# Front of an attention and feed-forward kernel: copies of v, weight passes and evictions placed anew, and ten unread products at the start

## The chip, the cores and the metric

The kernel runs on one NeuronCore of a Trainium2 chip. The metric is device time in microseconds (us) for one execution, from the first to the last instruction and a little around it. Less is better.

## What is computed

The reference is a thresholded attention, and behind it a feed-forward block with the SoLU activation:

```python
scores = (q @ k.T) / sqrt(64)                        # 8 batches, 8 heads, 576 x 576
thresh = max(scores, axis=-1) - tau                  # tau = 0.02
scores = where(scores >= thresh, scores, -1e9)
attn = softmax(scores)
x = (attn @ v)  ->  4608 tokens x 512
h = x @ w_in                                         # 512 x 1024
solu = h * softmax(h)
out = (layernorm(solu) * g_ln) @ w_out               # 1024 x 512
```

q, k and v are fp32. The weights w_in and w_out come as 64-bit floats, and the kernel turns them into fp32 itself.

## The kernel before

The kernel is one long program without loops on the chip; Python loops write it out. It goes in rounds. A round has one slot of the attention: 128 query rows against 576 keys, for each of two heads. Batch b has 18 slots (four pairs of heads, two kinds of rows and two halves of each, and two slots for the last 64 rows), so there are 144 rounds. Rounds 0 to 29 are the front; from round 30 (START) a steady order follows that works off attention and feed-forward side by side.

In a round, TensorE makes the scores into two PSUM tiles, s0 and s1, of which there is one each, so the scores of a round wait until ScalarE has read those of the round before. VectorE takes the row maxima (`maxes`, L526), ScalarE makes everything below the threshold vanish with a steep ramp (`ramp`, L541) and takes exponentials with row sums (`exps`, L550). In the round after, GpSimd divides by the sums (`normalise`, L557 to L560), VectorE transposes blocks of 32x32 (`blocks`, L571), and the SyncE queue moves the blocks into place (`spread`, tile wT, L592 to L601). Some rounds later TensorE multiplies them with v (L631); ScalarE copies the result to xh (L664).

Around this the front does three things:

- **The weights.** They come in 16 pieces (0 to 7 of w_in, 8 to 15 of w_out). Each goes through `weight_load` (into one of four raw buffers, RAW), `weight_a` (an exponent pass on the engine that UNIT names: 0 VectorE, 1 ScalarE, 2 GpSimd, L294 to L298; a sign pass on VectorE, L303; a low-word pass on ScalarE, L306), `weight_b` (VectorE, L318) and `weight_c` (an addition on GpSimd, L328). The pieces of w_out are also scaled by g_ln (`weight_gain`, engine by GAIN: 0 ScalarE, 1 VectorE, 2 GpSimd) and copied to swapped rows (`weight_d`, engine by MOVER: 0 ScalarE, 1 VectorE, 2 GpSimd, 3 a DMA).
- **q, k and v.** Each pair of heads of batches 0 and 1 is turned on TensorE by products with an identity (`turn`, L372) and evicted from PSUM. PREP says in which round the items of pairs 4 to 7 are turned, and EASED whether ScalarE does all the evictions of a round (1) or shares them with VectorE (0). Pairs of later batches are loaded in their natural form (LOAD2), transposed by VectorE (TURN2, L221) and moved by DMAs (L223). The rows of v of batch 0 are copied once to the other half of the partitions, in eight copies (`copy_v`; VAT says when, VBY on which engine: 0 ScalarE, L187; 1 VectorE; 2 GpSimd, L191). FETCH and V2 say when q, k and v are loaded.
- **Four tiles of the feed-forward block** in rounds 11 to 32 (HO gives the rounds of their products, CHAIN the places of the steps between: maximum, exponential, product, statistics, normalising in two halves, the swap DMAs, the transpose).

Each engine works through its instructions in the order of the program. That order is set by hand: a time in VAT, PIECE or MOVE is 4 times the round plus a phase. Phase 0 is before the scores of the round, 1 before the normalising, 2 before the feed-forward and attention products and the transposes, 3 at the round's end. `weigh` runs what is due at a phase; at one phase the additions come first, then `weight_b`, loads, `weight_a`, scalings, copies of weights, copies of v. In CHAIN a step has one of four places (begin, early, middle, late) and a number of rounds after its products.

A product with v becomes due three rounds after the second slot of its unit, plus LAG. Due ones stand in a list in order. In the front one is taken from its head in a round, under this condition, where `what` names the feed-forward steps of the round:

```python
if due and "o" not in what and len(pairs_free) > ("h" in what and steps[0][1] == 0):
    attending = pv_due.pop(0)[1]
```

The beginning is its own: the first loads, the constants, then the turning of pair 0 (k, a quarter of q and the ends) by `turned`, and round 0.

Of the kernel before, what the change touches and what calls it, by code (L numbers as in the profile page):

```python
# [8 lines left out]
F32 = mybir.dt.float32  # L9
# [11 lines left out]
def kernel(  # L21
# [937 lines left out]
    SPLIT = {30: 0, 32: 30, 34: 6, 36: 5, 38: 16, 40: 30, 42: 7, 44: 23, 46: 11}  # L959
    LATER, KEPT = 47, (3, 4)  # L960
    SEVEN = {0: 21, 1: 21, 2: 24, 3: 25, 5: 25, 4: 26, 7: 26, 6: 29}
    PIECE = {0: (-1, 1, 3, 6, 7, ), 1: (-1, 3, 5, 10, 11, ), 2: (-1, 8, 11, 14, 15, ), 3: (3, 12, 15, 18, 19, ), 4: (4, 15, 18, 21, 25, ), 5: (7, 20, 23, 26, 27, ), 6: (11, 23, 25, 30, 31, ), 7: (13, 27, 31, 34, 35, ), 8: (23, 31, 35, 38, 39, ), 9: (23, 35, 39, 42, 43, ), 10: (29, 39, 43, 46, 47, ), 11: (35, 43, 47, 50, 51, ), 12: (39, 49, 51, 54, 55, ), 13: (43, 52, 55, 58, 59, ), 14: (43, 55, 59, 62, 63, ), 15: (55, 59, 63, 66, 67, )}
# [4 lines left out]
    MOVER = {16: 0, 17: 0, 18: 2, 19: 1, 20: 2, 21: 0, 22: 3, 23: 3, 24: 0, 25: 0, 26: 3, 27: 3, 28: 3, 29: 2, 30: 3, 31: 3}  # L967
    MOVE = {8: 47, 9: 55, 10: 55, 13: 63, 14: 70, 15: 67}
    EASED = {0: 0, 1: 1, 2: 1, 3: 1, 4: 1, 5: 1, 6: 1, 7: 0, 8: 1, 9: 1, 10: 0, 11: 1, 12: 0, 13: 0, 14: 0, 15: 1, 16: 1, 17: 0, 18: 0, 19: 1, 20: 1, 21: 0}
    SECOND = {0: 0, 1: 1, 2: 0, 3: 1, (1, 0, 0): 1}  # L970
    PREP = {0: 14, 1: 14, 2: 14, 3: 15, 4: 15, 5: 17, 6: 16, 7: 16, 8: 19, 9: 19, 10: 18, 11: 20, 12: 20, 13: 22, 14: 21, 15: 21}
    LAG = {1: 2, 3: 1, 5: 1, 9: 1, 11: 1, 17: 0, 21: 0, 23: 1, 25: 1}
    FETCH = {0: 10, 1: 8, 2: 8, 3: 11, 4: 15, 5: 15, 6: 13, 7: 17, 8: 17, 9: 19, 10: 21, 11: 25, 12: 0, 13: 0, 14: 3, 15: 5}
# [3 lines left out]
    LOAD2 = {0: 20, 1: 17, 2: 24, 3: 21, 4: 31, 5: 31, 6: 32, 7: 34}  # L977
# [338 lines left out]
    with tc.manual_schedule():  # L1316
# [317 lines left out]
```

## Time and profile before

| | before |
|---|---|
| three runs | 845.42, 846.64, 848.91 us |
| median | 846.64 us |
| the profiled execution | 848.12 us |
| its span, first to last instruction | 846.3 us |
| mean granted TensorE clock | 0.983 |
| busy: TensorE, VectorE, ScalarE, GpSimd | 799.6, 674.5, 605.0, 574.2 us |

In the lines of the profile, PE is TensorE's matmuls, PEld its weight loads, DVE VectorE, ACT ScalarE, POOL GpSimd, SP SyncE, and a q behind the name is the engine's queue. A line of a timeline has the start and the duration in us, engine, source line, operation, the tile written and those read, the shape, the count, and in brackets how long the engine stood idle before it and what ended that. A matmul in fp32 counts as two. A line of the page about an engine's 40 slices shows the busy tenths of each.

### The profile page before, as it was taken

Reading aid. Unit: us, or ns where it says so; the run is one execution under the profiler, and the core shown is the slowest. Engines: PE = TensorE matmul, PEld = TensorE weight load, DVE = VectorE, ACT = ScalarE, POOL = GpSimd, SP = SyncE. Lnnn points to the kernel's source line nnn. Section 1 sums busy time; section 2 is a strip of 40 time slices with the busy share of each in tenths; the row PEclk is TensorE's granted clock in tenths of the full one; section 3 lists DMA queues with packets and bytes.
Section 4 is the critical chain, followed back from the end, with each engine's and each line's share of the span. In section 5 each row is a group of like instructions: output and inputs, shape, how many; then the busy total and the mean of one; then the engine's idle time right before and its main releaser. Section 6 shows DMA issues by size and latency. Waiting matters only on the chain.

```text
span 846.3 us, 36895 instructions
## 1 busy us (share of the span) xinstructions
PE 799.6 (94%) x15345; PEld 554.4 (66%) x15345; DVE 674.5 (80%) x1323; ACT 605.0 (71%) x1218; POOL 574.2 (68%) x1036
## 2 busy tenths in 40 slices
PE   5569889999999999999999999999999999999997
PEld 3346667766665666666777876666676876666556
DVE  5799869878789698979798698979688888787362
ACT  6799868767777686878686787778586687876231
POOL 4979767866867667677766768686666768574330
PEclk9789999999999999999999999999999999999999
DMA  8989788988787687968787677877687666555122
GB/s 252 256 219 253 189 204 212 236 222 211 220 244 216 174 224 211 242 190 218 205 230 208 195 207 220 231 206 199 192 218 222 180 183 201 150 138 139 42 52 52
DMA packets 99768, 166.40 MB, mean 197 GB/s; under 512 B 18504, under 2 KB 47184, under 8 KB 99600
## 3 DMA queue, kind: packets, MB, share of 16 engines
q1 hardware_dynamic: 98688, 162.95, 71.1%
q8 instruction: 121, 1.98, 1.0%
q10 hardware_dynamic: 912, 1.08, 0.5%
q14 instruction: 47, 0.39, 0.1%
HBM read 45.09 MB, written 9.44 MB: 64 GB/s over the span
## 4 chain that ended last, share of the span: by engine, by line
PE 82%; ACT 5%; POOL 3%; DMA 3%; issue 3%; DVE 2%; SPq 1%; DVEq 0%; POOLq 0%; ACTq 0%
PE ov L1195 22%; PE h L747 17%; PE s_ps L504 15%; PE ov L631 13%; PE o_ps L1195 6%; PE h L771 5%; ACT w L541 2%; PE h_ps L1061 2%; DMA wT<-T 2%; DMA v<-in_v_dram 1%; ACT w L550 1%; POOL w L560 1%; PE pv L631 1%; DVE w L526 1%; PE s_ps L372 1%
## 5 line engine op out<-in xcount | busy, mean ns | idle before, releaser
L541 ACT ACTIVATE w<-s_ps,nth 128x576 f32<-128x576 f32 x282 | 199.6, 741 | 141.4 <-DVE nth L526 136.2
L526 DVE CUSTOM_DVE_ANT_0 w<-s_ps,tau_t 128x576 f32<-128x576 f32 x282 | 201.4, 750 | 51.8 <-PE s_ps L504 40.7
L560 POOL TENSOR_SCALAR w<-w,sm 128x576 f32<-128x576 f32 x288 | 214.6, 757 | 14.3
L1195 PE MATMUL ov<-w,uT 64*64 64x256 f32 x3456 | 220.5, 379 | 2.8 <-issue 2.8
L571 DVE STREAM_TRANSPOSE T<-w 128x576 f32<-128x576 f32 x288 | 207.4, 755 | 19.2 <-POOL w L560 18.4
L550 ACT ACTIVATE w<-w,ntau 128x576 f32<-128x576 f32 x288 | 219.7, 768 | 0.0
L504 PE MATMUL s_ps<-kT,qT 64*64 64x512 f32 (+1 forms) x2048 | 174.8, 418 | 20.1 <-ACT w L541 17.9
L1195 PEld LDWEIGHTS ov<-w,uT 64*64 64x64 f32 x3456 | 158.3, 134 | 49.1 <-issue 13.6
L631 PEld LDWEIGHTS ov<-wT,v 64*64 64x64 f32 x4752 | 132.6, 133 | 33.5 <-issue 18.7
L631 PE MATMUL ov<-wT,v 64*64 64x128 f32 (+1 forms) x4752 | 137.6, 259 | 0.2
L557 POOL TENSOR_SCALAR sm<-sm 128x2 f32<-128x2 f32 x144 | 45.9, 319 | 134.9 <-ACT w L550 130.3
L558 POOL TENSOR_TENSOR sm<-sm,mone 128x2 f32<-128x2 f32 x144 | 103.5, 719 | 12.0
L504 PEld LDWEIGHTS s_ps<-kT,qT 64*64 64x64 f32 x2048 | 72.0, 137 | 51.0 <-ACT w L541 23.7
L747 PE MATMUL h<-w,xh 64*64 64x512 f32 x832 | 103.4, 593 | 0.5 <-POOL mark L110 0.4
L1150 DVE TENSOR_SCALAR u<-u,rs,nb 128x1024 f32<-128x1024 f32 x31 | 29.8, 961 | 49.6 <-ACT V L1144 49.6
L1195 PE MATMUL o_ps<-w,uT 64*64 64x256 f32 x1088 | 65.5, 377 | 0.8 <-ACT xh L664 0.5
L747 PEld LDWEIGHTS h<-w,xh 64*64 64x64 f32 x832 | 38.6, 133 | 40.5 <-issue 23.1
L1195 PEld LDWEIGHTS o_ps<-w,uT 64*64 64x64 f32 x1088 | 49.1, 133 | 19.1 <-issue 5.2
L550 ACT ACTIVATION_READ_ACCUMULATOR w<-w,ntau 128x1 f32 x288 | 55.7, 193 | 0.0
L1177 DVE STREAM_TRANSPOSE uT<-V 128x1024 f32<-128x1024 f32 x36 | 44.0, 1221 | 14.2 <-DMA V<-u 4.9
L747 PE MATMUL h<-k,sum 64*64 64x512 f32 x312 | 50.6, 589 | 0.0
L1144 ACT ACTIVATE V<-u,nb,rs 128x1024 f32<-128x1024 f32 x36 | 44.7, 1241 | 5.2 <-POOL nb L1122 5.2
(134 smaller groups left out, 1017.0 us busy)
## 6 DMA issues: line engine op xcount, KB each, us to landing
wT<-T SPq DMA_DIRECT2D x132, 288.0 KB, 4.8
wT<-T SPq DMA_DIRECT2D x256, 144.0 KB, 4.0
out_dram<-ob SPq DMA_DIRECT2D x71, 128.0 KB, 4.3
V<-u SPq DMA_DIRECT2D x136, 64.0 KB, 2.0
wT<-T SPq DMA_DIRECT2D x14, 576.0 KB, 5.5
q<-in_q_dram SPq DMA_DIRECT2D x24, 288.0 KB, 4.6
q<-in_k_dram SPq DMA_DIRECT2D x24, 288.0 KB, 4.5
v<-in_v_dram SPq DMA_DIRECT2D x12, 576.0 KB, 5.6
```

Of the source, the lines that this page charges most:

```text
L504: nc.tensor.matmul(out=ps[h][ROWS[y], ks], lhsT=lhsT, rhs=d["kT"][ROWS[h], ks], start=True, stop=True,)
L526: nc.vector.tensor_tensor_reduce(out=w, in0=ps[:, 0:S], in1=(zero if loose else tau_t).to_broadcast([P, S]), scale=1.0, scalar=BIG, op0=AL ...
L541: nc.scalar.activation(out=d["w"][x], in_=d["w"][x] if d["loose"] else d["ps"][x][:, 0:S], func=AF.Prelu, bias=d["nth"][x], scale=-1.0, al ...
L550: nc.scalar.activation(out=w, in_=w, func=AF.Exp, bias=ntau, scale=1.0, accum_out=sm[:, x : x + 1])
L557: nc.gpsimd.tensor_scalar(out=sm, in0=sm, scalar1=1e-9, scalar2=None, op0=ALU.add)
L558: nc.gpsimd.tensor_tensor(out=sm, in0=sm, in1=mone, op=ALU.pow)
L560: nc.gpsimd.tensor_scalar(out=w, in0=w, scalar1=sm[:, x : x + 1], scalar2=1.0, op0=ALU.mult, op1=ALU.mult)
L571: nc.vector.transpose(out=T[:, :, r, :, h, :], in_=w.rearrange("p (c m x) -> p c m x", c=2, x=32))
L631: nc.tensor.matmul(out=to, lhsT=d["v"][ROWS[u], (h0 + h - u) % 4 if b > 1 else h0 + h, m ^ 4 * u if m < 8 and b < 2 else m,], rhs=rhs, sta ...
L747: mm = nc.tensor.matmul(out=h[ROWS[y], 512 * bank : 512 * bank + 512], lhsT=x[ROWS[r], ROWS[y]], rhs=w[ROWS[r]], start=c == 0 and (n, r, k ...
L1144: nc.scalar.activation(out=V, in_=u, func=AF.Identity, bias=nb, scale=rs)
L1195: nc.tensor.matmul(out=to[ROWS[z], 0:256], lhsT=d["uT"][ROWS[r], m].rearrange("p y x -> p (y x)"), rhs=w2[ROWS[r], m ^ r, 256 * z : 256 * ...
```

## The change

Nothing is computed otherwise, and no instruction of the attention or the feed-forward block is added or taken away. The tables that place the front's side work get other values, and ten products are added at the start. Part by part:

- **Ten unread products.** VectorE clears a tile of 128x128 ahead of the constants (in a buffer of tag T). TensorE multiplies it with itself, into s0, seven times ahead of the first turning and three times between the first turning and the scores of round 0. Nobody reads the results.
- **Copies of v.** Copies 0 to 7 stood at times 15, 15, 19, 19 (GpSimd) and 31, 31, 34, 34 (ScalarE). Now 0 and 2 are VectorE's at the beginning of rounds 3 and 4, 1 is ScalarE's in round 2, 3 stays GpSimd's in round 3, 4 is GpSimd's at the end of round 8, and 5, 6 and 7 are ScalarE's in rounds 8, 7 and 8.
- **Weight passes.** The exponent passes of pieces 0, 14 and 15 go from VectorE to GpSimd, those of 6 and 8 from ScalarE to GpSimd, that of 5 from GpSimd to VectorE, that of 11 from ScalarE to VectorE. The scaling of piece 8 goes from VectorE to GpSimd, that of 9 from ScalarE to VectorE, that of 10 from VectorE to ScalarE. One swapped-row copy goes from ScalarE to GpSimd (21) and one from GpSimd to ScalarE (29). Several passes change their phase: the addition of piece 1 goes ahead of the normalising of round 1, the passes b of pieces 3, 5, 8 and 11 ahead of the transposes of their rounds, the load of piece 6 from round 2 to 3, of piece 10 from round 7 to 6, and the copies of pieces 8, 9 and 10 some phases forward.
- **q and k.** Two items of pair 5 are turned in rounds 13 and 14 instead of 15 and 17, one of pair 6 in round 21 instead of 18, one of pair 7 in round 19 instead of 20. Rounds 15, 16, 19 and 20 share their evictions between ScalarE and VectorE; round 13 has them on ScalarE.
- **Loads.** The loads of k of pair 5 and q of pair 4, of v of batch 1 (second half, 21 to 25) and of batch 2, and the natural loads and transposes of batch 2 move by some rounds.
- **Products with v.** LAG makes those after slots 3, 11, 21 and 23 due two, two, one and two rounds earlier.
- **The chains of the first feed-forward tiles.** Some steps move by one place or one round; the store of the first goes from round 19 to 21, the swap of the second's halves from round 20 to the end of 19, and the transpose of the fourth from round 31 to 32.

```diff
+    BEFORE, BESIDE = 7, 3
...
-    UNIT = {0: 0, 1: 2, 2: 2, 3: 2, 4: 1, 5: 2, 6: 1, 7: 1, 8: 1, 9: 0, 10: 1, 11: 1, 12: 1, 13: 1, 14: 0, 15: 0}
-    GAIN = {8: 1, 9: 0, 10: 1, 11: 0, 12: 2, 13: 0, 14: 0, 15: 2}
+    UNIT = {0: 2, 1: 2, 2: 2, 3: 2, 4: 1, 5: 0, 6: 2, 7: 1, 8: 2, 9: 0, 10: 1, 11: 0, 12: 1, 13: 1, 14: 2, 15: 2}
+    GAIN = {8: 2, 9: 1, 10: 0, 11: 0, 12: 2, 13: 0, 14: 0, 15: 2}
...
-    VAT = {0: 15, 1: 15, 2: 19, 3: 19, 4: 31, 5: 31, 6: 34, 7: 34}
-    VBY = {0: 2, 1: 2, 2: 2, 3: 2, 4: 0, 5: 0, 6: 0, 7: 0}
+    VAT = {0: 12, 1: 9, 2: 16, 3: 15, 4: 35, 5: 32, 6: 29, 7: 34}
+    VBY = {0: 1, 1: 0, 2: 1, 3: 2, 4: 2, 5: 0, 6: 0, 7: 0}
...
+        rest = work.tile([P, 2, 2, NK, 2, 32], F32, tag="T", name="rest")
+        still = rest.rearrange("p c r m h x -> p (c r m h x)")[:, 0:P]
+        nc.vector.memset(still, 0.0)
+        idle = ps_mm.tile([P, 1024], F32, tag="s0", name="idle")
+
+        def idle_products(n):
+            for _ in range(n):
+                nc.tensor.matmul(
+                    out=idle[:, 0:P], lhsT=still, rhs=still, start=True, stop=True
+                )
+
+        idle_products(BEFORE)
         constants()
...
         turned(first, [k_item(0), q_item(0, slice(0, 1)), e_item(0)])
+        idle_products(BESIDE)
```

The other tables, old to new, only the entries that differ (a piece with all five times: load, a, b, c, scaling; the copies have the fifth time too, or that of MOVE):

```text
PIECE  1: (-1,3,5,10,11) -> (-1,3,5,9,11); 3: (3,12,15,18,19) -> (3,12,14,18,19)
       5: (7,20,23,26,27) -> (7,20,21,26,27); 6: (11,23,25,30,31) -> (13,24,25,30,32)
       8: (23,31,35,38,39) -> (23,31,34,38,39); 10: (29,39,43,46,47) -> (27,39,43,46,47)
       11: (35,43,47,50,51) -> (35,43,46,50,51); 12: (39,49,51,54,55) -> (39,50,51,55,55)
       13: (43,52,55,58,59) -> (43,51,54,56,56)
MOVE   8: 47 -> 43; 9: 55 -> 53; 10: 55 -> 52        MOVER  21: 0 -> 2; 29: 2 -> 0
EASED  4, 8, 15, 16, 19, 20: 1 -> 0; 10, 13: 0 -> 1
PREP   4: 15 -> 13; 5: 17 -> 14; 10: 18 -> 21; 12: 20 -> 19
LAG    3: 1 -> -1; 11: 1 -> -1; 21: 0 -> -1; 23: 1 -> -1
FETCH  1: 8 -> 9; 2: 8 -> 11; 10: 21 -> 25; 15: 5 -> 6
LOAD2  0: 20 -> 18; 1: 17 -> 20; 5: 31 -> 29; 6: 32 -> 29; 7: 34 -> 35
TURN2  1: 24 -> 25; 3: 28 -> 30; 4: 33 -> 34; 5: 34 -> 38
V2     0: 21 -> 22; 1: 27 -> 24; 2: 32 -> 37; 3: 35 -> 40
CHAIN  2: (3,1) -> (0,2); 9: (3,1) -> (3,3); 13: (3,3) -> (2,3); 16: (1,6) -> (3,5);
       19: (0,1) -> (1,1); 25: (3,2) -> (0,3); 29: (3,1) -> (2,2); 32: (3,1) -> (1,1);
       37: (1,6) -> (3,7); 39: (2,2) -> (3,1)
```

More of the change, by code (lines that the diff above doesn't have):

```diff
@@ L970 @@
+    MOVE = {8: 43, 9: 53, 10: 52, 13: 63, 14: 70, 15: 67}
+    EASED = {0: 0, 1: 1, 2: 1, 3: 1, 4: 0, 5: 1, 6: 1, 7: 0, 8: 0, 9: 1, 10: 1, 11: 1, 12: 0, 13: 1, 14: 0, 15: 0, 16: 0, 17: 0, 18: 0, 19: 0, 20: 0, 21: 0}
     SECOND = {0: 0, 1: 1, 2: 0, 3: 1, (1, 0, 0): 1}
-    PREP = {0: 14, 1: 14, 2: 14, 3: 15, 4: 15, 5: 17, 6: 16, 7: 16, 8: 19, 9: 19, 10: 18, 11: 20, 12: 20, 13: 22, 14: 21, 15: 21}
-    LAG = {1: 2, 3: 1, 5: 1, 9: 1, 11: 1, 17: 0, 21: 0, 23: 1, 25: 1}
-    FETCH = {0: 10, 1: 8, 2: 8, 3: 11, 4: 15, 5: 15, 6: 13, 7: 17, 8: 17, 9: 19, 10: 21, 11: 25, 12: 0, 13: 0, 14: 3, 15: 5}
+    PREP = {0: 14, 1: 14, 2: 14, 3: 15, 4: 13, 5: 14, 6: 16, 7: 16, 8: 19, 9: 19, 10: 21, 11: 20, 12: 19, 13: 22, 14: 21, 15: 21}
```

16 lines of the change are left out of this document (8 added, 8 removed).

## The prediction

> **What bounds the kernel now.** I read first the page: its span, its busy shares and its 40 slices.
>
> ```profile
> span 846.3 us, 36895 instructions
> PE 799.6 (94%) x15345; PEld 554.4 (66%) x15345; DVE 674.5 (80%) x1323; ACT 605.0 (71%) x1218; POOL 574.2 (68%) x1036
> PE   5569889999999999999999999999999999999997
> ```
>
> TensorE is busy 94% of the span, and all of its idleness that can be won back is in the first four slices (85 us). The change touches rounds 0 to about 40 only, most of it rounds 0 to 22, so the question is how much sooner the front hands over to a stretch in which TensorE is already full. Second view: the windows, by engine.
>
> ```profile
> 30.00:40.00 10.00, 6.02 (x76) 3.97 (x78) 5.60 (x12) 8.55 (x21) 9.21 (x14) 0.66 0.88 235
> 50.00:60.00 10.00, 6.25 (x104) 4.26 (x104) 9.04 (x19) 9.88 (x21) 7.36 (x10) 0.83 0.86 216
> 140.00:150.00 10.00, 10.00 (x198) 7.17 (x194) 8.70 (x16) 7.59 (x15) 9.38 (x13) 1.00 0.60 135
> 150.00:160.00 10.00, 10.00 (x204) 8.98 (x199) 8.26 (x17) 7.34 (x15) 8.85 (x16) 1.00 1.06 248
> ```
>
> The columns behind the width are PE, PEld, DVE, ACT, POOL, granted clock, DMA share, GB/s. From 30 to 40 us GpSimd is the full engine (9.21) and VectorE is idle by nearly half; from 50 to 60 ScalarE is full (9.88); from 140 on it is TensorE. Three stretches, three limits.
>
> Third view: the timelines of rounds 1 to 7, engine by engine. In a round the ramp on ScalarE (L541) waits for the maxima (L526) on VectorE, these for the scores (L504) on TensorE, and the scores for the ramp of the round before, which frees their banks. VectorE runs in order, and ahead of the maxima of round r+1 it has the transposes (L571) of round r-1, which wait for GpSimd's normalising (L557 to L560).
>
> ```profile
> 24.68 1.42 ACT L541 ACTIVATE w<-s_ps,nth 128x576 f32<-128x576 f32 x2
> 34.53 1.41 ACT L541 ACTIVATE w<-s_ps,nth 128x576 f32<-128x576 f32 x2
> 42.55 1.42 ACT L541 ACTIVATE w<-s_ps,nth 128x576 f32<-128x576 f32 x2 [4.01 <-DVE nth L526]
> 38.82 1.50 DVE L571 STREAM_TRANSPOSE T<-w 128x576 f32<-128x576 f32 x2 [3.75 <-POOL w L560]
> 41.71 0.74 DVE L526 CUSTOM_DVE_ANT_0 w<-s_ps,tau_t 128x576 f32<-128x576 f32 x1
> 27.68 1.69 POOL L191 TENSOR_SCALAR v<-v 64x512 f32<-64x512 f32 x2
> 33.52 1.35 POOL L191 TENSOR_SCALAR v<-v 64x512 f32<-64x512 f32 x2
> 34.95 0.65 POOL L298 TENSOR_SCALAR em<-raw 128x512 f32<-128x512 f32 x1
> 35.99 2.19 PE L504 MATMUL s_ps<-kT,qT 64*64 64x64 f32 x12 [0.15 <-ACT w L541]
> ```
>
> The ramps of rounds 3, 5 and 6 start at 24.68, 34.53 and 42.55: round 6 is 8.0 us after round 5, where rounds 3 to 5 took 4.9 each. Round 6 had its scores by 38.2 (35.99 + 2.19), but its maxima began at 41.71, behind transposes that stood 3.75 us for GpSimd, and that was late because it had copied v four times (1.69 + 1.35) and run a weight pass (0.65) since 27.68.
>
> **The start (ten products).** Seven products of 128x128 run while TensorE waits for k, three while it waits for the first evictions.
>
> ```profile
> 3.58 1.19 PE L372 MATMUL tp<-ident,k 64*64 64x64 f32 x31 [3.58 <-DMA k<-in_k_dram]
> 6.19 2.20 PE L504 MATMUL s_ps<-kT,qT 64*64 64x64 f32 x16 [0.98 <-DVE kT L451]
> 48.30 1.24 PE L504 MATMUL s_ps<-kT,qT 64*64 64x64 f32 x16
> 12.79 0.92 DVE L303 TENSOR_SCALAR em<-raw 128x512 int32<-128x512 int32 x1 [1.53 <-DMA raw<-in_moe_w_in_dram]
> 10.11 0.42 DVE L303 TENSOR_SCALAR em<-raw 128x512 int32<-128x512 int32 x1
> 15.07 1.45 ACT L541 ACTIVATE w<-s_ps,nth 128x576 f32<-128x576 f32 x2
> ```
>
> The same 16 scores take 2.20 us in round 0 and 1.24 in round 8, so a TensorE that is at full clock by 6.2 us saves up to 0.96; one that is not saves nothing, and the products may then delay the first turning (idle until 3.58) by some tenths. I take 0.5 gained, bounds 1.0 gained to 0.4 lost. It gets through to the ramp of round 1 (15.07), but no more than 0.6 would: the maxima of that round stand behind a pass that waits for raw weights until 12.79 and takes 0.92, so the first of them (0.74) is done at 14.4 at best. The Trainium skill ("TensorE: Matmul & The Clock Gate", What's actually happening) says the clock follows activity in free-running windows of about 3.4 us, whatever the kernel's start. By that the gain would be 0 or nearly 1 from run to run, and one run cannot tell which; the two L504 rows agree with a clock of half and of full.
>
> **Rounds 2 to 5, a loss.** The addition of weight piece 1 on GpSimd (L328) moves ahead of the normalising of round 1, and a copy of v each goes to VectorE ahead of the maxima of rounds 3 and 4.
>
> ```profile
> 18.72 0.23 POOL L557 TENSOR_SCALAR sm<-sm 128x2 f32<-128x2 f32 x1
> 21.30 1.28 POOL L328 TENSOR_TENSOR w<-w,em 128x512 int32<-128x512 int32 x1
> 23.83 0.74 DVE L526 CUSTOM_DVE_ANT_0 w<-s_ps,tau_t 128x576 f32<-128x576 f32 x1
> ```
>
> Normalising runs from 18.72 to 21.30; 1.28 in front make that 22.6. VectorE then still has one transpose (0.75), the scaling and sign passes it had before (together 1.7, from 22.1 to 23.83), and a copy, which I price as the nearest VectorE pass, 0.42 alone, 0.92 beside GpSimd: 22.6 + 0.75 + 1.7 + 0.42 = 25.5 for the maxima instead of 23.83, and the ramp of round 3 about 26.2 instead of 24.68, 1.5 later. ScalarE has its copy of v (0.62, half of the row at 51.19 below) in that hole. v should be there: its load is issued at 14.26 and such loads land in 5.6 us. In rounds 4 and 5 the loop recovers a little; I carry 1.2 late at the ramp of round 5 (bounds 0.5 and 2.0).
>
> ```profile
> 14.26 0.37 SPq L174 DMA_DIRECT2D v<-in_v_dram  x1
> v<-in_v_dram SPq DMA_DIRECT2D x12, 576.0 KB, 5.6
> 51.19 1.25 ACT L187 COPY v<-v 64x512 f32<-64x512 f32 x2
> 49.95 0.67 ACT L294 ACTIVATE em<-raw 128x512 f32<-128x512 f32 x1
> ```
>
> **Round 6, the gain.** GpSimd loses three of four copies and the pass of piece 5: 1.69 + 1.35 + 0.65 less about 0.75 for the copy that stays is 2.9, less the 1.3 of above that it starts late. Its normalising of round 4 then ends ahead of the scores of round 6 and is no longer what is late. Late is the loop itself: ramp of round 5 at 34.53 + 1.2 = 35.7, done at 37.1, scores 2.2 at half clock to 39.3, first maximum 0.7, ramp at 40.0 instead of 42.55. Round 6 stands 2.5 ahead. The Trainium skill ("SBUF — State Buffer", Who interferes with whom) says that VectorE's two-port passes and GpSimd lock each other out for a whole instruction; this speaks against moving copies from one to the other. The two L303 rows agree (0.42 alone, 0.92 beside GpSimd); by the rule the two copies would block GpSimd for 2 x 0.42, and the 2.9 would be 2.1, which would still put the scores last.
>
> **Rounds 7 to 11.** ScalarE is full here. It loses the exponent passes of pieces 6, 8 and 11 (0.67 each), the scaling of piece 9 and one copy of v (0.62) to GpSimd and VectorE, which have room (7.36 and 9.04 of 10). Up to the ramp of round 10 that is 0.67 + 0.62, of which I let 0.9 count: 3.4 ahead. Then TensorE waits for transposed weights:
>
> ```profile
> 62.26 1.98 PE L631 MATMUL pv<-wT,v 64*64 64x128 f32 x64 [0.87 <-DMA wT<-T]
> 51.98 1.50 DVE L571 STREAM_TRANSPOSE T<-w 128x576 f32<-128x576 f32 x2
> 54.82 7.40 DMA wT<-T
> ```
>
> These are transposed from 51.98, sent, and on their way 7.40 us. In the new order VectorE first scales piece 8, and I get the transposes done at 51.8 instead of 53.5, 1.7 sooner; two loads less in front (piece 10 earlier, q and k of pairs 4 and 5 later) may add 0.4. So the products start 2.1 sooner and 1.3 of the 3.4 is given back. From here rounds 11 to 13 are TensorE's, which carries the 2.1. Bounds: 1.0 (no help from the loads, transposes half as early) and 3.4 (not late at all).
>
> **Rounds 12 to 20.** GpSimd takes two exponent passes and a transposed copy more, but starts ahead; I count -0.1. The evictions of turned q and k go from ScalarE alone to both engines in rounds 15, 16, 19 and 20 (EASED), and fewer are made in rounds 15 and 17.
>
> ```profile
> 91.80 0.50 ACT L408 ACTIVATE qT<-s_ps,scl 128x256 f32<-128x256 f32 x1
> 94.55 1.51 PE s_ps L504 x8
> 86.85 1.60 issue
> 121.67 1.83 issue
> ```
>
> Each eviction that leaves ScalarE is 0.3 to 0.5 between two ramps; three fewer in round 15, two in 16, three in 20 are some 2.5. TensorE waits only part of that, so I take 1.5 (bounds 0 and 2.6). Two gaps of TensorE that nothing shown ends (1.60 and 1.83 in the chain of waits) I leave in place. Front 1's second normalised half is sent a position sooner, which frees VectorE near 121, but TensorE stands in the second of these gaps there: nothing.
>
> **Rounds 21 to 40.** The earlier due dates (LAG) move no product with v: products leave a queue in order, one a round, not in a round with output products and not without a free bank pair, and after these rules all go in the rounds in which they go now. New is 512 KB of v loaded in round 25 instead of 21, ahead of the transposed weights for round 29:
>
> ```profile
> 152.92 1.76 SPq L174 DMA_DIRECT2D v<-in_v_dram  x2
> 165.62 2.07 PE L631 MATMUL pv<-wT,v 64*64 64x128 f32 x66 [0.82 <-DMA wT<-T]
> 170.02 1.95 PE L771 MATMUL h<-w,xh 64*64 64x512 f32 x16 [0.59 <-POOL w L704]
> 173.39 0.65 PE L771 MATMUL h<-w,sum 64*64 64x512 f32 x2 [1.42 <-POOL sum L723]
> ```
>
> At the 248 GB/s of that window this is 2.1 us more in front. TensorE waits there already, and next it waits 0.59 and 1.42 for GpSimd, which take up 2.0 of it. I take 0.3 lost. The later loads of batch 2 and the later turning of front 3 I count at nothing: they have a round or more before use.
>
> **Sum.** 2.1 ahead at round 11, -0.1, +1.5, -0.3: 3.2 us sooner. The profiled execution took 848.12 us (1.8 outside its span), which makes 844.9; it is 1.5 above the median of 846.64, so the forecast is 843.4. About 0.5%, 4.2 us, is what a measurement of this kernel can tell from no change.
>
> **The rivals.**
> *The front gives everything.* The ScalarE evictions are worth their 2.6, and with a steadier TensorE the eight scores at 94.55 run at the pace of the sixteen at 48.30, which halves their 1.51, and one of the two chain gaps goes (1.6). That is 3.2 + 1.1 + 0.7 + 1.6 = 6.6, or 840.0. For it: sixteen scores took less than these eight. Against: the gaps have no releaser that the change touches.
> *It is hidden anyway.* The transposed weights at 62.26 are as late as now but for 0.5, and TensorE from there on is full: 846.1. For it: the 7.40 of transfer isn't touched. Against: the transposes are surely sooner if round 6 is.
> *Slower, by the loads in front of round 29.* In rounds 24 and 25 stand then 512 KB of v, 288 KB of v from round 27 and the turned q from round 24. At 248 GB/s 1.1 MB is 4.5 us. If TensorE's two later gaps don't take it up, and the front brings only the 1.0 of its lower bound without evictions, the time is 846.6 + 4.5 - 1.0 = 850.1. It decides once the weights for round 29 land later by more than the front has won, 3.5 us by my sum. For it: DMA is full at 150 to 160 (1.06). Against: it is at 0.60 ten us before, and the 288 KB fit there.
>
> **How the numbers follow.** Forecast 0.45, everything 0.24, hidden 0.14, slower 0.17. The forecast's own range, 840.7 to 846.0, has a third below 842.4: 0.15; with the second case faster is 0.39. Of the slower case 0.10 lies above 850.9, at its own price or beyond; same is the rest, 0.51. A range from 838.7 to 849.6 leaves out about 0.1 on each side.
>
> **What would show it.** Right: the ramp of round 6 near 40 with VectorE's wait for L560 under 1.5; the ramp of round 3 near 26, later than now; round 0's scores near 1.3 if the clock was up; products of round 10 starting near 60. Wrong: a ramp of round 6 after 42, ScalarE waiting for a copy of v in round 2, or TensorE's wait before the products of round 29 above 4 us.

## The result, and the profile after

The changed kernel is slower: 856.81 us median of six runs (850.39 to 858.32) against 846.44 us of six runs of the kernel before (845.38 to 848.91). The ratio is 1.0093, 95% interval 1.0065 to 1.0122, or 8 us; the two medians lie 10.4 us apart. Prices below go by ratios where a ratio stands beside them. The forecast was 843.4 us, its range ended at 849.6. A second set beside other kernels gave 856.06 us and 1.0101 (1.0060 to 1.0141).

The profiled execution took 853.09 us. First its page: the span, the busy shares, TensorE's slices.

```profile
span 851.3 us, 36939 instructions
PE 803.7 (94%) x15365; PEld 542.1 (64%) x15365; DVE 675.2 (79%) x1331; ACT 603.0 (71%) x1208; POOL 581.3 (68%) x1039
PE   7669889889899999999999999999999999999997
```

The first slices are fuller than before (7669 where 5569 stood); of the 4.1 us that TensorE is busy longer, 3.8 are in the first slice, where the ten products run. What to look at is further right: the eighth, ninth and eleventh slices (149 to 192 and 213 to 234 us) are emptier, 8 where 9 stood. The windows of the front still look better: from 50 to 60 us ScalarE is down from 9.88 to 8.40 and TensorE up from 6.25 to 7.12.

```profile
30.00:40.00 10.00, 5.71 (x78) 3.51 (x74) 8.87 (x18) 8.42 (x21) 8.95 (x12) 0.67 0.96 272
50.00:60.00 10.00, 7.12 (x116) 4.77 (x120) 9.08 (x17) 8.40 (x17) 9.27 (x12) 0.83 0.86 217
```

The timeline of ScalarE has the ramps of rounds 3, 5 and 6, that of TensorE the first turning, the scores of round 0 and the first long products with v:

```profile
24.98 1.42 ACT L541 ACTIVATE w<-s_ps,nth 128x576 f32<-128x576 f32 x2 [0.33 <-DVE nth L526]
35.41 1.42 ACT L541 ACTIVATE w<-s_ps,nth 128x576 f32<-128x576 f32 x2 [0.60 <-DVE nth L526]
39.87 1.42 ACT L541 ACTIVATE w<-s_ps,nth 128x576 f32<-128x576 f32 x2 [0.98 <-DVE nth L526]
```

```profile
4.32 1.13 PE L372 MATMUL tp<-ident,k 64*64 64x64 f32 x32
7.31 1.21 PE L504 MATMUL s_ps<-kT,qT 64*64 64x64 f32 x16
59.77 2.07 PE L631 MATMUL pv<-wT,v 64*64 64x128 f32 x66 [0.81 <-DMA wT<-T]
```

Round 6 starts at 39.87 instead of 42.55, the products at 59.77 instead of 62.26. So the front was sooner by about what was forecast. To see where it is lost, one instruction that every round has, the first exponential (L550), is compared round by round. Rounds 20 and 42, before and then after:

```profile
120.41 0.81 ACT L550 ACTIVATE w<-w,ntau 128x576 f32<-128x576 f32 x1
232.34 0.77 ACT L550 ACTIVATE w<-w,ntau 128x576 f32<-128x576 f32 x1
```

```profile
116.70 0.78 ACT L550 ACTIVATE w<-w,ntau 128x576 f32<-128x576 f32 x1
237.63 0.77 ACT L550 ACTIVATE w<-w,ntau 128x576 f32<-128x576 f32 x1
```

Round 20 is 3.7 us ahead, round 42 is 5.3 behind: 9 us lost in 22 rounds, and one more by round 108. The differences in us (a minus is ahead of the kernel before), for the changed kernel and for six of the experiments below, each from its one profiled execution:

```text
round                        3     6    20    21    24    30    31    33    40    42    60   108
after                      0.3  -2.7  -3.7  -0.8  -0.6   2.7   0.8   3.3   3.3   5.3   5.6   6.3
1 load tables back        -0.1  -3.1  -3.2  -1.4  -1.8  -1.1  -1.1   0.7   0.7   0.7   1.7   2.9
2 load tables alone       -0.3  -0.6   0.1   0.9   1.0   4.8   2.9   4.0   4.1   7.8   9.4  11.2
4 passes and copies only   1.0  -1.9  -0.8  -0.7  -0.7  -0.7  -0.7  -0.7  -0.7   0.0  -0.2   0.9
7 products alone          -1.1  -1.2  -2.5  -2.5  -2.2  -1.7  -1.7   0.3   0.3   0.5   0.6   1.2
8 loads, chain back        1.2  -1.8  -3.0  -2.4  -2.4  -2.2  -2.2  -1.1  -1.1  -1.4  -0.7   0.6
10 as 8, no products       0.5  -2.5  -2.7  -3.0  -2.9  -2.7  -2.7  -2.7  -2.4  -2.0  -2.2  -1.5
```

(From round 111 to 114 all seven fall by 2.4 to 3.4: there the profiled execution of the kernel before itself loses time, by a gap of TensorE of 2.05 us at 597.45 and a granted clock of 0.59 from 600 to 604 us, so the table ends at 108.)

One execution is not the kernel: a second profiled execution of the changed kernel (experiment 12) is 2.1 ahead in round 18 and only 0.9 in round 20, and 6.1 behind in round 42.

The steps at rounds 21, 30, 33 and 41 are TensorE's waits in its timeline:

```profile
116.69 1.21 PE L631 MATMUL pv<-wT,v 64*64 64x64 f32 x66 [0.62 <-DMA wT<-T]
121.95 0.38 PE L631 MATMUL pv<-wT,v 64*64 64x64 f32 x9 [2.22 <-issue]
166.60 0.43 PE L631 MATMUL pv<-wT,v 64*64 64x128 f32 x4 [2.77 <-DMA wT<-T]
167.60 3.54 PE L631 MATMUL pv<-wT,v 64*64 64x128 f32 x66 [0.57 <-DMA wT<-T]
185.86 1.76 PE L631 MATMUL ov<-wT,v 64*64 64x128 f32 x56 [1.58 <-DMA wT<-T]
225.06 2.15 PE L631 MATMUL ov<-wT,v 64*64 64x128 f32 x60 [1.01 <-ACT w L541]
```

Two kinds are here. In rounds 29 to 41 TensorE waits for transposed weights: 2.77 + 0.57 where the kernel before waits 0.69 + 0.82, then 1.58 and 1.01 where it does not wait. (The last is put down to a ramp; experiment 6 makes it likely that the weights are what came late.) In round 21 it stands 2.22 us for nothing that the profile shows; the kernel before stands there too, 1.83 us.

SyncE's queue in front of round 29, after and then before:

```profile
150.21 0.71 SPq L157 DMA_DIRECT2D v<-in_v_dram  x1
153.31 1.95 SPq L174 DMA_DIRECT2D v<-in_v_dram  x3
155.30 1.27 SPq L179 DMA_DIRECT2D v<-in_v_dram  x2
156.68 0.59 SPq L592 DMA_DIRECT2D wT<-T  x1
```

```profile
156.12 0.59 SPq L592 DMA_DIRECT2D wT<-T  x1
161.12 1.21 SPq L223 DMA_DIRECT2D kT<-flip  x2
162.37 0.60 SPq L157 DMA_DIRECT2D v<-in_v_dram  x1
```

The 288 KB of v (L157) went behind the weights; now they go in front of them, with the 512 KB that also moved there (the third of L174; at 152.92 in the kernel before there were two). The weights are issued only 0.56 later, but the last of them land 2 later (167.56 instead of 165.58).

### The profile page after: what moved, and what is told of

The parts are those of the page before. It is cut to its first block, busy times and chain, and to the rows that moved or that the text cites. A ratio compares the mean times of both kernels' runs of the same rounds, so it can differ in the third digit from the quotient of the medians.

```text
span 851.3 us, 36939 instructions
## 1 busy us (share of the span) xinstructions
PE 803.7 (94%) x15365; PEld 542.1 (64%) x15365; DVE 675.2 (79%) x1331; ACT 603.0 (71%) x1208; POOL 581.3 (68%) x1039
## 3 DMA queue, kind: packets, MB, share of 16 engines
q8 instruction: 121, 1.98, 1.0%
## 4 chain that ended last, share of the span: by engine, by line
PE 72%; DMA 7%; POOL 5%; ACT 4%; DVE 4%; issue 3%; SPq 3%; DVEq 0%; POOLq 0%; ACTq 0%
PE ov L1196 19%; PE h L747 17%; PE s_ps L504 12%; PE ov L631 12%; PE o_ps L1196 6%; DMA wT<-T 4%; PE h L771 2%; POOL w L560 2%; PE h_ps L1062 2%; ACT w L550 2%; ACT w L541 2%; PE pv L631 1%; POOL w L328 1%; DVE w L526 1%; DVE T L571 1%
## 5 line engine op out<-in xcount | busy, mean ns | idle before, releaser
L560 POOL TENSOR_SCALAR w<-w,sm 128x576 f32<-128x576 f32 x288 | 217.8, 768 | 14.3
L550 ACT ACTIVATE w<-w,ntau 128x576 f32<-128x576 f32 x288 | 219.5, 766 | 0.0
L1196 PE MATMUL ov<-w,uT 64*64 64x256 f32 x3456 | 210.9, 376 | 1.3 <-ACT xh L664 0.9
L504 PE MATMUL s_ps<-kT,qT 64*64 64x512 f32 (+1 forms) x2048 | 165.6, 417 | 18.8 <-ACT w L541 16.9
L1196 PEld LDWEIGHTS ov<-w,uT 64*64 64x64 f32 x3456 | 148.3, 133 | 54.9 <-issue 14.5
L631 PEld LDWEIGHTS ov<-wT,v 64*64 64x64 f32 x4752 | 129.0, 133 | 43.7 <-issue 23.9
L504 PEld LDWEIGHTS s_ps<-kT,qT 64*64 64x64 f32 x2048 | 64.3, 137 | 52.8 <-ACT w L541 23.3
L1196 PE MATMUL o_ps<-w,uT 64*64 64x256 f32 x1088 | 66.9, 377 | 1.4 <-DMA w<-w 1.2
L1151 DVE TENSOR_SCALAR u<-u,rs,nb 128x1024 f32<-128x1024 f32 x31 | 27.9, 901 | 50.2 <-ACT V L1145 50.2
L1196 PEld LDWEIGHTS o_ps<-w,uT 64*64 64x64 f32 x1088 | 56.9, 133 | 12.5 <-issue 3.2
L747 PEld LDWEIGHTS h<-w,xh 64*64 64x64 f32 x832 | 35.2, 133 | 44.1 <-issue 28.1
L550 ACT ACTIVATION_READ_ACCUMULATOR w<-w,ntau 128x1 f32 x288 | 55.4, 192 | 0.0
```

Source lines behind the costliest of these rows:

```text
L504: nc.tensor.matmul(out=ps[h][ROWS[y], ks], lhsT=lhsT, rhs=d["kT"][ROWS[h], ks], start=True, stop=True,)
L550: nc.scalar.activation(out=w, in_=w, func=AF.Exp, bias=ntau, scale=1.0, accum_out=sm[:, x : x + 1])
L560: nc.gpsimd.tensor_scalar(out=w, in0=w, scalar1=sm[:, x : x + 1], scalar2=1.0, op0=ALU.mult, op1=ALU.mult)
L631: nc.tensor.matmul(out=to, lhsT=d["v"][ROWS[u], (h0 + h - u) % 4 if b > 1 else h0 + h, m ^ 4 * u if m < 8 and b < 2 else m,], rhs=rhs, sta ...
L747: mm = nc.tensor.matmul(out=h[ROWS[y], 512 * bank : 512 * bank + 512], lhsT=x[ROWS[r], ROWS[y]], rhs=w[ROWS[r]], start=c == 0 and (n, r, k ...
L1196: nc.tensor.matmul(out=to[ROWS[z], 0:256], lhsT=d["uT"][ROWS[r], m].rearrange("p y x -> p (y x)"), rhs=w2[ROWS[r], m ^ r, 256 * z : 256 * ...
```

## The experiments

The first theory was the slower rival of the prediction: the moved loads (FETCH, LOAD2, TURN2, V2) eat the front's lead. Its rivals: the ten products, or a front that brings nothing. Each ratio is against runs of the kernel before on the same chip; medians of the kernel before were 848.12, 847.07, 846.15 and 847.50 us in the four sets.

**1. Load tables back.** After with the four tables of before. (Here and below, changed entries of tables are written as assignments. In kernels that have the products or their table, the lines far down in the source have numbers one higher: L1196 is L1195, L1165 is L1164.)

```diff
-    FETCH[1], FETCH[2], FETCH[10], FETCH[15] = 9, 11, 25, 6
+    FETCH[1], FETCH[2], FETCH[10], FETCH[15] = 8, 8, 21, 5
-    LOAD2[0], LOAD2[1], LOAD2[5], LOAD2[6], LOAD2[7] = 18, 20, 29, 29, 35
+    LOAD2[0], LOAD2[1], LOAD2[5], LOAD2[6], LOAD2[7] = 20, 17, 31, 32, 34
-    TURN2[1], TURN2[3], TURN2[4], TURN2[5] = 25, 30, 34, 38
+    TURN2[1], TURN2[3], TURN2[4], TURN2[5] = 24, 28, 33, 34
-    V2[0], V2[1], V2[2], V2[3] = 22, 24, 37, 40
+    V2[0], V2[1], V2[2], V2[3] = 21, 27, 32, 35
```

> The changed kernel with the four tables that place loads and natural transposes (FETCH, LOAD2, TURN2, V2) as before; all else changed. Loads theory (the moved transfers stand in front of transposed weights in rounds 29, 33 and 41, worth 5 to 6 us, and in the runs that are slower than the profiled one more): 1 to 4 us faster than before, TensorE's waits for wT after 160 us back to about 1.5 us. Rival, the new order of turnings, evictions and feed-forward steps in rounds 13 to 22: still 3 us or more slower than before. Rival, the ten products: still about 8 slower.

849.56 us, ratio 1.0031 (1.0012 to 1.0050). 5.2 us come back; the steps at rounds 30 and 41 are gone from the table, the one at 33 is not. The time is still 2.6 above the kernel before, not the 1 to 4 below that the loads theory expected, so something else costs as well.

**2. Load tables alone.** Before with only those four tables changed: the diff of 1 read from + to -.

> The kernel before with only those four tables changed. Loads theory: 5 to 10 us slower than before. Both rivals: within 1.5 us of before.

853.87 us, 1.0074 (1.0051 to 1.0098). Put in, the four tables cost 6.3 us; taken out, 5.2 come back. The place is as clear: the four profiled executions that have the tables (after, 2, 3 and 12) lose 3.2 to 3.9 us from round 29 to 30, of which 1.3 to 2.0 are left in round 31, and 2.0 to 3.7 from round 40 to 42. The ten others with all four tables as before lose at most 1.3 and 1.5 there.

**3. No products.** After without the ten products.

```diff
-    BEFORE, BESIDE = 7, 3
+    BEFORE, BESIDE = 0, 0
```

> The changed kernel without the ten unread products (the clearing of the tile stays). Loads theory and order theory: as slow as the changed kernel within 2 us, if anything 0.5 slower for round 0. Theory of the products (their instructions and the clock harm what follows): back to within 2 us of before.

851.47 us, 1.0051 (1.0027 to 1.0074). This is some 3.6 us below after, with intervals that overlap a little: the products seem to cost something, where the prediction had them gain half a microsecond. It is neither within 2 us of after nor of before, so neither theory has it all.

**4. Passes and copies alone.** Before with PIECE, UNIT, GAIN, MOVER, MOVE, VAT and VBY of after.

```diff
-    UNIT, GAIN, VAT, VBY = ...  # of before
+    UNIT, GAIN, VAT, VBY = ...  # and PIECE, MOVER, MOVE, as the change has them
```

> The kernel before with only the tables of weight passes and copies changed (PIECE, UNIT, GAIN, MOVER, MOVE, VAT, VBY). If the GpSimd relief holds as in the changed kernel's trace: ramp of round 6 about 2.5 us sooner, whole kernel 1.5 to 3 us faster than before. If what the front wins is always given back before TensorE is full: within 1 us of before.

845.22 us, 0.9976 (0.9958 to 0.9995): 2 us below the kernel before, a small difference, but the interval lies below 1.

**5. Half of v later.** Before with one entry changed.

```diff
-    FETCH[10] = 21
+    FETCH[10] = 25
```

> The kernel before with one entry of FETCH changed: the second half of v of batch 1 (512 KB) is loaded in round 25 instead of 21. Loads theory: the transposed weights for round 29 land 2 to 3 us later; the exponentials of round 30 start 2 to 4 us later than in the kernel before, TensorE's two later gaps (0.59 and 1.42 us) take up to 2.0 of that, and the end is 1 to 3 us later. Prediction's theory (2.1 us absorbed but for 0.3): the end moves by less than 0.5 us. Noise theory (the loss was gaps of TensorE that come and go): no difference at round 30.

**9. Both loads of v.** The same, and with it the L157 row above.

```diff
-    FETCH[10], V2[1] = 21, 27
+    FETCH[10], V2[1] = 25, 24
```

> The kernel before with two entries changed: the second half of v of batch 1 (FETCH 10) in round 25 instead of 21, and the first 512 KB-sized load of batch 2 after it (V2 1, a load of 288 KB) in round 24 instead of 27. Theory: it is the pair that puts the weights for round 29 late. The 288 KB go out near 150 us, ahead of them, instead of near 162 us behind them; at the 245 to 265 GB/s of that stretch this is 1.1 to 1.2 us more than FETCH 10 alone (weights 0.7 us later there), so the weights land near 167.5 instead of 165.6, the exponentials of round 30 start 2 to 3 us later, and 0 to 1.5 us of it are left in round 31 and at the end. Rival (only the whole set of moved loads does it): as with FETCH 10 alone, less than 1 us at round 30.

TensorE's timeline at round 29, of 5 and then of 9:

```profile
164.92 0.44 PE L631 MATMUL pv<-wT,v 64*64 64x128 f32 x4 [1.30 <-DMA wT<-T]
166.31 2.07 PE L631 MATMUL pv<-wT,v 64*64 64x128 f32 x66 [0.95 <-DMA wT<-T]
```

```profile
165.95 0.44 PE L631 MATMUL pv<-wT,v 64*64 64x128 f32 x4 [1.40 <-DMA wT<-T]
167.31 3.34 PE L631 MATMUL pv<-wT,v 64*64 64x128 f32 x66 [0.92 <-DMA wT<-T]
```

Alone, the 512 KB make the wait 0.7 longer, and round 31 no later: 0.54 ahead in round 29, 0.52 in 31. In that execution the prediction's small price for this edit holds, and the 2 to 4 us expected at round 30 were too much (0.5). With the 288 KB as well the products start at 167.31, as expected, round 30 goes from 0.7 ahead to 2.6 behind, and 1.4 are left in round 31. Of those 3.4 us, 1.27 are the same 66 products running for 3.34 instead of 2.07. TensorE also waits for the late v itself there, a little earlier in its timeline of 9:

```profile
161.39 2.07 PE L631 MATMUL pv<-wT,v 64*64 64x128 f32 x66 [1.51 <-DMA v<-in_v_dram]
```

That it takes the pair is not shown. Experiment 6 below moves neither load, and its one profiled execution waits at the same place, goes from 0.6 ahead to 2.0 behind in round 30 and has 0.8 left in round 31:

```profile
165.47 0.44 PE L631 MATMUL pv<-wT,v 64*64 64x128 f32 x4 [1.70 <-ACT w L550]
166.79 2.75 PE L631 MATMUL pv<-wT,v 64*64 64x128 f32 x66 [0.89 <-DMA wT<-T]
```

The times do not tell the pair from its half either: 5 has 849.76 us, ratio 1.0031 (1.0005 to 1.0058), 9 has 849.13, 1.0026 (1.0002 to 1.0050). By the ratio the 512 KB alone cost 2.6 us (0.4 to 4.9), more than the 0.3 of the prediction; but the median of 5 lies 4 us above its own profiled execution (845.72), and its runs spread from 845.4 to 853.9, and the trace shows no place for the difference.

**6. Turns later.** Before with two natural transposes later.

```diff
-    TURN2[3], TURN2[5] = 28, 34
+    TURN2[3], TURN2[5] = 30, 38
```

> The kernel before with two entries of TURN2 changed: natural transposes 3 and 5 of batch 2, with the DMAs that move their blocks, in rounds 30 and 38 instead of 28 and 34. Loads theory: SyncE's queue sends the transposed weights of rounds 33 and 41 behind these DMAs (about 0.6 us each to issue), so TensorE waits for wT in rounds 33 and 41 and the end is 3 to 5 us later. Rival (what counts is the bytes, which are the same, and the 512 KB of v): within 1 us of the kernel before.

849.05 us, 1.0018 (0.9998 to 1.0037). The time is unclear, the place is not: round 41 goes from 1.0 to 3.3 behind. TensorE, then SyncE's queue; below that the same weights in the kernel before:

```profile
223.67 0.44 PE L631 MATMUL ov<-wT,v 64*64 64x128 f32 x4 [1.91 <-ACT w L541]
```

```profile
210.26 2.77 SPq L223 DMA_DIRECT2D kT<-flip  x2
218.21 1.19 SPq L223 DMA_DIRECT2D qT<-flip  x2
219.50 0.57 SPq L592 DMA_DIRECT2D wT<-T  x1
```

```profile
215.29 0.57 SPq L592 DMA_DIRECT2D wT<-T  x1
```

The queue is in order: two moves of turned k stand in it for 2.77 us, two of q take 1.19, and the weights go out at 219.50 instead of 215.29. The bytes are the same as before; it is the place in the queue that decides here. In round 33, where a wait was expected too, only 0.3 was lost.

**7. Products alone.** Before with the ten products.

```diff
+        idle_products(BEFORE)
...
+        idle_products(BESIDE)
```

> The kernel before with the ten unread products and nothing else. Prediction's theory: scores of round 0 at full clock, exponentials of rounds 0 to 2 0.3 to 0.6 us sooner, the end within 1 us of the kernel before. Rival (the products cost what the removed loads do not explain: the order of everything on the other engines shifts and a wait falls elsewhere): 2 to 3 us slower.

850.05 us, 1.0022 (0.9999 to 1.0045), by the interval unclear. The profiled execution gains 1.2 in the front, is 1.65 ahead at round 32, and loses 1.94 in round 33 alone. TensorE, then SyncE's queue there, and below the queue of before:

```profile
182.90 1.76 PE L631 MATMUL ov<-wT,v 64*64 64x128 f32 x56 [1.71 <-DMA wT<-T]
```

```profile
169.76 3.26 SPq L1165 DMA_DIRECT2D V<-u  x4
173.13 0.62 SPq L592 DMA_DIRECT2D wT<-T  x1
```

```profile
171.59 2.49 SPq L1164 DMA_DIRECT2D V<-u  x4
174.19 0.62 SPq L592 DMA_DIRECT2D wT<-T  x1
```

The weights of round 33 go out behind four moves of u, 1.06 sooner only, and what is left of the lead becomes a wait. In this stretch the front can hand its lead on no further than the transposed weights are ahead as well.

**8. Loads and chain back.** After with FETCH, LOAD2, TURN2, V2, LAG and CHAIN of before: the diff of 1, and

```diff
-    CHAIN[2], CHAIN[9], CHAIN[16], CHAIN[19], CHAIN[37] = (0, 2), (3, 3), (3, 5), (1, 1), (3, 7)
+    CHAIN[2], CHAIN[9], CHAIN[16], CHAIN[19], CHAIN[37] = (3, 1), (3, 1), (1, 6), (0, 1), (1, 6)
...
```

> The changed kernel with FETCH, LOAD2, TURN2, V2, LAG and also CHAIN as in the kernel before. If the later steps of the first feed-forward tiles (CHAIN) cost what was left over with the load tables alone put back, the loss in round 33 (2.0 us there) is gone and the time is 1 us below to 1 us above the kernel before. If the transposed weights of round 33 bind whatever is done in front of them, round 33 takes back 2 us again and the time is 2 to 3 us above, as with the load tables alone.

847.42 us, 1.0019 (0.9998 to 1.0039). From round 32 to 33 it loses 1.05 where experiment 1 lost 2.0; the time is 1 us below that of 1, with intervals that overlap. This lies between the two cases expected. That CHAIN costs about 1 is likely, not shown.

**10. The same without products.** 8 without the ten products and the clearing of their tile, so 4 with EASED and PREP.

> The changed kernel without the ten products and with FETCH, LOAD2, TURN2, V2, CHAIN and LAG as before: the moves of weight passes and copies (the version that was 2 us faster than before) plus EASED and PREP. If the products cost something, this comes out 1 us or more below the same kernel with them, and 1 to 2 us below the kernel before. If EASED and PREP cost it, it stays level with the kernel before.

844.98 us, 0.9976 (0.9958 to 0.9995). This is the case in which the products cost something: 3.6 us below 8, with intervals that do not meet.

**11. Passes, copies and products.** 4 with the ten products (the diff of 7).

> The kernel before with the moves of weight passes and copies (PIECE, UNIT, GAIN, MOVER, MOVE, VAT, VBY) and the ten products. If the products are worth their half microsecond at the end, 2 to 3 us below the kernel before. If the lead of the front ends at the transposed weights of round 33, which SyncE's queue sends 16 DMA issues after those of round 31, the products add nothing: 1 to 2 us below at most, with a wait for wT in round 33 that is longer by what the front is sooner.

850.68 us, 1.0041 (1.0019 to 1.0064). The lead ends in round 33 (from 0.2 ahead to 1.35 behind), but that explains 1.5; against 4 it is slower by 5.5 (1.0041 against 0.9976). Neither of the two cases expected has a time above the kernel before.

**12. After again**, unaltered.

> The changed kernel once more, unaltered, to stand beside the others on the same chip. Its profile should lose to the kernel before at rounds 21, 29 to 30, 33 and 41 again, 8 us from round 20 to 42, and the time should be 5 to 10 us above; a part of the loss that does not return (the gap of TensorE in round 21) is no part of the change.

856.06 us, 1.0101 (1.0060 to 1.0141); the steps at rounds 30, 33 and 41 are there again (3.8, 1.6 and 3.7), in round 21 only 0.5 is lost. The loss from round 20 to 42 is 7.0, where 8 was expected.

So the products cost 3.6 us (3 against after), 3.6 (10 against 8), 5.5 (4 against 11) and 1.9 (7, unclear): in 8 and 11 more than the 1.05 and 1.5 lost in round 33. From 235 us on, gaps of TensorE that nothing shown ends stand only inside output products (L1195) in kernel 10, and in front of other matmuls in kernel 8; one row of 10, then two of 8:

```profile
405.21 2.10 PE L1195 MATMUL ov<-w,uT 64*64 64x256 f32 x33 [1.68 <-issue]
```

```profile
405.91 0.40 PE L631 MATMUL ov<-wT,v 64*64 64x64 f32 x12 [1.17 <-issue]
697.86 0.66 PE L504 MATMUL s_ps<-kT,qT 64*64 64x512 f32 x4 [0.51 <-issue]
```

All gaps over 0.15 us from 235 us on add up to 3.7 us in kernel 10 and 5.2 in kernel 8. The page of after shows two queues for instructions, a small one (46 packets) and this one:

```profile
q8 instruction: 121, 1.98, 1.0%
```

1.98 MB in 121 packets are 16.4 KB each; TensorE's 30,730 matmuls and weight loads make 254 a packet, some 64 bytes each. Ten fp32 products are 40 of them. If this queue brings TensorE's program, they shift every later packet against the work. The Trainium skill ("Runtime: NRT & Kernel Launch", Instruction fetch mechanics) says that instructions are fetched in blocks of 16 KiB, 256 instructions, and that crossing a block is mostly hidden; the packet size agrees, and so does the small number of gaps, three to seven over 0.3 us in a kernel behind 60 us (counted below), but some are over 2 us long. Three kernels tell the shift from the products' work: 10 with ten, 32 and 64 small products in one place. By the shift 64, a whole packet, is as good as none.

```diff
+    BEFORE = 10    # 13;  32 in 14;  64 in 15
...
+                nc.tensor.matmul(out=idle[0:32, 0:32], lhsT=still[:, 0:32], rhs=still[:, 0:32], ...)
```

**13. Ten small products.**

> The changed kernel with FETCH, LOAD2, TURN2, V2, CHAIN and LAG as before, and in place of the seven and three products of 128x128 ten products of 32 columns, all in one place. Instruction theory: ten products are 40 instructions of TensorE; its program comes in packets of 16 KB (1.98 MB in 121 packets, about 254 instructions each), so every later packet begins at another matmul, and the gaps that no releaser ends fall where they fall with ten large products: near 406, 599, 698 us before products with v and scores, none in the output products L1195, 2 us more idle time from 235 us on than without products, and the time 2 to 3.5 us above the same kernel without. Rival (what costs is the products' own work or heat at the start): like the kernel without products.

**14. Half a packet.**

> The same with 32 small products, 128 instructions, half a packet. Instruction theory: the gaps stand at yet other places and the time differs from both, by up to 5 us either way; no sign is forecast. Rival: the time grows with the number of products, from ten over 32 to 64.

**15. A whole packet.**

> The same with 64 small products, 256 instructions, a whole packet of 16 KB. Instruction theory: every later packet begins where it begins without products, the gaps come back to the output products L1195 near 405 and 597 us, and the time is that of the kernel without products, plus 0 to 1.5 us if the 64 products delay the first turning. Rival: the time grows with the number of products, and this is the slowest of the three.

**16. None, again** (kernel 10).

> The kernel without products again, beside the three on one chip: 1 to 3.5 us below the kernel before, gaps without a releaser in L1195 alone from 235 us on.

| products | median, us | ratio to before |
|---|---|---|
| none (16) | 844.69 | 0.9975 (0.9959 to 0.9992) |
| ten (13) | 850.87 | 1.0043 (1.0022 to 1.0064) |
| 32 (14) | 856.23 | 1.0129 (1.0092 to 1.0166) |
| 64 (15) | 846.55 | 0.9987 (0.9969 to 1.0004) |

The time does not grow with the products: by the medians 64 cost 1.9 (1.0 by the ratios, whose intervals overlap), 32 cost 11.5, ten 6.2. So the products' own work is not what costs. With 64 the time is about the 0 to 1.5 expected; with ten it is more than the 2 to 3.5 expected, with 32 more than the 5 either way. The page of 15 has one packet more in that queue, as 256 more instructions of TensorE need:

```profile
q8 instruction: 122, 2.00, 1.1%
```

TensorE's timelines, for none, 64, 32 and ten:

```profile
404.98 2.10 PE L1195 MATMUL ov<-w,uT 64*64 64x256 f32 x33 [0.91 <-issue]
596.94 2.15 PE L1195 MATMUL ov<-w,uT 64*64 64x256 f32 x33 [1.18 <-issue]
```

```profile
409.78 2.85 PE L1196 MATMUL ov<-w,uT 64*64 64x256 f32 x33 [2.12 <-issue]
602.96 2.15 PE L1196 MATMUL ov<-w,uT 64*64 64x256 f32 x33 [0.72 <-issue]
```

```profile
317.34 2.10 PE L1196 MATMUL ov<-w,uT 64*64 64x256 f32 x33 [1.89 <-issue]
509.66 2.15 PE L1196 MATMUL ov<-w,uT 64*64 64x256 f32 x33 [1.62 <-issue]
702.01 2.16 PE L1196 MATMUL ov<-w,uT 64*64 64x256 f32 x34 [1.69 <-issue]
```

```profile
602.23 0.40 PE L631 MATMUL ov<-wT,v 64*64 64x64 f32 x11 [1.01 <-issue]
```

With a whole packet the gaps are back where they are without products, the same 33 products in front of the same two output products; with half a packet they stand elsewhere, three of 1.6 to 1.9 us; with ten, two of the three places expected show one (602 us, and 0.22 us at 701), the one near 406 shows none. In 16 there is also one in front of scores (0.55 us at 631.52), where L1195 alone was expected.

A count settles the place. In the eighteen traces there are 93 gaps of TensorE over 0.3 us, behind 60 us, that nothing shown ends. Counted in matmuls from the start of the program, 89 of them stand within three matmuls of a grid of 126.9 matmuls (254 matmuls and weight loads, one packet); by chance it would be some five. A gap with 1873 to 1875 matmuls ahead of it is in seventeen of the traces, with none, ten or 64 products; with 32 it is at 1748 and 2002. With 5429 to 5431 ahead it is there with ten and 32, with 7206 or 7207 with none and ten, with 7335 with 64. So a gap stays at its packet while the program moves past it, and which packets show one depends on the work that stands there.

What the shift costs is less clear than where it acts. The gaps from 235 us on are 1.5 us longer in kernel 8 than in 10, for 3.6 us of time. They are 8.3 us with 32 products, 5.1 with 64, 2.9 with ten and 3.1 with none, so with ten they are not the 2 us longer that were expected. Kernel 13 loses in the front instead: in the profiled executions it is 0.3 behind kernel 16 at round 6, 3.7 at round 24, 5.8 at round 42 and 6.5 at the end. How gaps and waits there add up to this is open.

## Why the prediction was wrong, point by point

- **Start, 0.5 gained.** The scores of round 0 took 1.21 (about 1.3 was named) instead of 2.20, as at full clock; the trace itself does not list a half clock there (granted 1.00 from 0 to 10 us in the kernel before), only the durations differ. But the products stand in front of the first turning, which starts at 4.32 instead of 3.58. So the scores start at 7.31 instead of 6.19, and the exponentials of rounds 0 and 1 are only 0.2 ahead (0.9 in experiment 7, 1.1 and 0.6 in 12). The step that failed here is the price: the ten products were priced by their own time, between 1.0 gained and 0.4 lost, and cost 1.9 to 5.5 at the end, by the shift of TensorE's program. The two gaps "that nothing shown ends" were in the prediction, left in place; one of them, 1.83 in front of turned products, became the 2.22 in front of products with v, 1873 and 1875 matmuls from the start. Their cause was the thing to ask for.
- **Rounds 2 to 6.** Right, with VectorE's transposes no longer waiting for GpSimd in front of round 6. Ramp of round 5 at 35.41 (35.7 forecast), of round 6 at 39.87 (40.0). The loss in round 3 was overestimated: its ramp came at 24.98 (26.2 forecast); 0.3 late, 1.1 in experiment 12.
- **Rounds 7 to 11.** Right in the number, 2.5 ahead at the products (2.1; 1.6 in experiment 12), not in the path. The lead was 3.2 in round 8 and 2.1 in round 10 already, not 3.4; and the waits for wT grew by 0.4 (1.54 + 0.81 instead of 1.12 + 0.87), not by 1.3.
- **Rounds 12 to 20.** The number came out in one execution: 3.7 ahead in round 20, where 2.1 - 0.1 + 1.5 = 3.5 was said. In the other it was 0.9, so this is in part luck. EASED and PREP account for 1.9 of it there (10 against 4, one execution each), though the medians of the two cannot be told apart.
- **Rounds 21 to 40, 0.3 lost.** Wrong by 5 to 6 us, the largest miss. "The later loads of batch 2 and the later turning of front 3 I count at nothing" is the failed step: the four tables cost 6.3 us put in and 5.2 taken out. One of these loads was not later but sooner, in front of the weights of round 29, and the turnings were looked at for their own use, not for what stands behind them in SyncE's queue. The 512 KB alone moved nothing in the trace of experiment 5; its time leaves that open. In the rivals the 288 KB were named, and let go because DMA is at 0.60 ten us earlier; in the changed kernel it is at 0.82 there.
- **That the lead gets through to the end.** Not asked. What kernel 10 gained, 2.7 at round 20, was worth 2 us in the time (10 and 16), and with products 1.05 to 1.94 of it ends at the weights of round 33 (8, 11, 7).
- **LAG moves no product.** Right: with LAG alone put back the program has the same instructions in the same order on every engine.
- **The slower rival** had part of the mechanism, late weights behind moved loads in round 29, and a price of 850.1. Its mark, a wait of TensorE of over 4 us before round 29, did not come (3.34): the loss was spread over rounds 29, 33 and 41, and over the products.

The sum of what was measured, each by its ratio and as if the parts added: -2.0 for passes, copies, evictions (0.9976), +6.3 for the load tables (1.0074), +3.6 for the products (1.0051 to 1.0093), about +1 for CHAIN, together 8.9; the change measured 7.9 and 8.5. Kernel 10, without load tables, CHAIN, LAG and products, lies below both, by 2 us in two sets: 844.98 and 844.69, ratios 0.9976 and 0.9975.

Open: why single runs of one kernel spread by 8 us here, how the shift becomes time in the front, and which of LOAD2, TURN2 1 and 4 and V2 make up what is left of the load tables' 5 to 6 us beside experiments 6 and 9. A hint on the first: the profiled execution of 15 is the slowest of its twelve (848.69 us, the fastest 843.30), and behind its gap of 2.12 us the granted clock was 0.58 from 411 to 415 us.

## What to carry to other kernels

Price a moved DMA by what stands behind it in its queue, not by its own due time: look up the next transfer that a full engine waits for, and count issues and bytes in front of it. A lead won upstream is worth only as much as the tightest transfer downstream lets through. And instructions added at the very start of TensorE's program moved every instruction packet after them here: before such an edit is judged, run it once with the added instructions padded to a whole packet, which separates the edit from the shift. Look at a second profiled execution before a lead of a microsecond or two is called won.

## What the hardware showed unexpectedly

- Gaps of TensorE of 0.3 to 2.3 us that nothing shown releases stand at boundaries of its 16 KB instruction packets (89 of 93), three to seven of some 120 boundaries in a kernel; moving the boundaries by half a packet cost 11.5 us in 845.
- In the changed kernel a wait of 2.77 us took the clock with it: the granted clock was 0.71 from 166 to 169 us and 0.73 from 169 to 172, and the 66 products behind it ran 3.54 instead of 2.07. After 1.30 and 0.95 (experiment 5) they did not, after 1.40 and 0.92 (9) they did, at 3.34. The Trainium skill ("TensorE: Matmul & The Clock Gate", What's actually happening) gives an idle window of about 3.4 us for the fall to half clock, running freely; here shorter idle stretches were enough, and two nearly equal ones had different outcomes, which fits windows that run freely.
- The gaps at packets can take the clock as well: behind 2.05 us in the kernel before it was 0.59 from 600 to 604 us, behind 2.12 us in 15 it was 0.58 from 411 to 415 us.
- A DMA takes SyncE some 0.6 us to issue (1.19 for two, 0.57 to 0.62 for one), so ten more in front of a transfer would be some 6 us, an estimate from these rows.
